# A fused FFT and gated layer on one core: unread products ahead of the tables, another order of the first phase, a padded E row, and joins between VectorE's two products

## The chip, the core and the metric

The kernel runs on one core of a Trainium2 chip. The metric is the device time of one execution in microseconds. The time before is 1947.34 us, the median of 3 runs (1947.0 to 1948.01). Engines are called TensorE (PE in the profile; PEld is its weight load), VectorE (DVE), ScalarE (ACT), GpSimd (POOL) and SyncE (SP, which issues most DMAs here).

## The reference

```python
# x: (8, 3008, 256) float32; weights float64 as numpy makes them: gate, val (256, 1536), out (1536, 256)
X = np.fft.fft(np.fft.fft(x, axis=1), axis=2).real.astype(np.float32)
x = X.reshape(24064, 256)
gate = 1.0 / (1.0 + np.exp(-(x @ w_gate)))
val = x @ w_val
out = (gate * val @ w_out).astype(np.float32)
```

## The kernel before

**What it computes.** The real part of the two-dimensional transform is cos·cos minus sin·sin. The kernel takes the sums over the 3008 rows as products with cosine and sine tables (`stab`), and folds the transform over the 256 columns (`dtab`) into the weights. Rows `k` and `3008 - k` share the same sums, so only 1505 positions are computed, as `pk` (cosine sums of the folded columns), `qk` (sine sums) and one row `E` (cosine sums of the middle column, 128). All matmuls are float32, and each shows as two records in the trace.

**The first phase (L767 to L817, batch 0).** SyncE issues the loads in this order: two weight pieces, the two halves of `x`, the four pieces of the tables (cosine for `q` 0 to 2 and 3 to 5, then the sines), then weight pieces 2, 3, 5, 6, 8, 9, 4 and 7. The weights arrive as 64-bit floats. `weight_parts` (L299, L300 on ScalarE), `weight_join` (L309, L310 and L312 on VectorE, then L314 on GpSimd) turn a piece into float32. `merge` multiplies a piece of `w_gate` or `w_val` with `dtab` on TensorE (tile `ps`), and ScalarE copies the result to `G2` and `G1` (L334, L335). Small DMAs take the first row of `G2` to `ge` (L337). VectorE folds `x` (`fold_ops`, L391 to L404). TensorE then makes the cosine sums in two blocks of positions (tiles `ev` and `od`, blocks 0 and 1), the sums of E (`pe`) and the sine sums. For each block `then` copies `ev` to SBUF on ScalarE (L493), and `places` adds and subtracts on VectorE (L498, L501). For E, L550, L551 and L556 on ScalarE and four instructions on VectorE build `er`, which goes to memory (`ed`, L560).

**The loop (L883 on).** It has 576 tiles: 8 batches, 6 chunks of up to 252 positions, 12 blocks of 128 hidden units. The order of all instructions is written out by hand (a manual schedule). In step `i`:

- `front_a(i)`: TensorE adds `G1`·`pk` for gate and value to a PSUM bank `pf`. For `i` below 5 it also adds E by a product of one row (`G2[0:1]` with `er`, L608); for later tiles ScalarE has written `ge`·E into the bank first (`seed`, L599).
- `gate_a(i-1)`: the first sigmoid (L628) and the values of the mirrored positions, `z` (L629).
- `part(i)`: ScalarE saves twice the bank (L614, tile `ae`).
- `gate_b(i-1)`: VectorE's first product (L641), the second sigmoid (L642) and VectorE's second product (L643), which releases the bank; later GpSimd adds blocks of `h` (L649).
- the lists `pre[i]` (joins of a piece, then `weight_parts` of the next) and `use[i]` (`merge` on TensorE), for `i` up to 12.
- `back`, from `i` = 5 on: TensorE multiplies a finished block with `w_out` (tile `po`).
- `front_b(i)`: TensorE adds `G2`·`qk` to the bank, after L614 has read it.

There are three PSUM banks for `pf`; five others hold `po`, and in the first phase `ev`, `od`, `pe` and most `ps`. The joins of a step stand behind that step's second product; `insert(0, ...)` makes piece 4 precede piece 10 in step 4, and piece 7 precede piece 11 in step 5:

```python
        if i:
            gate_b(i - 1)
        for f in pre.pop(i, []) + use.pop(i, []):
            f()
```

The products of `merge` with piece 10 stand in step 5, between `front_a(5)` and the first `back`. The tile `wqk` (tag "qk") is the second buffer of the tag of `qk`; until batch 1 needs it, it holds weight pieces 3 and 5.

Of the kernel before, what the change touches and what calls it, by code (L numbers as in the profile page):

```python
# [82 lines left out]
def kernel(  # L83
# [10 lines left out]
    nc = tc.nc  # L94
    B, _, _, _, D = xf.shape
    F = moe_w_gate.shape[1]
    P = 128
# [8 lines left out]
    CH = 252  # L106
    NB = 1 + max(b // 3 for b in PLACE)
    WC = 256
# [12 lines left out]
    pqp = ctx.enter_context(tc.tile_pool(name="pqp", bufs=2))  # L121
# [12 lines left out]
    def mm(o, l, r, start, stop):  # L134
        nc.tensor.matmul(o, l, r, start=start, stop=stop, skip_group_check=True)  # L135

    def bank(name, other=None):
        if other is not None:
            return pso.tile([P, 512], F32, name=name, tag=f"po{other}")
        return psx.tile([P, 512], F32, name=name, tag="x")  # L140
# [37 lines left out]
    dt = const.tile([P, 2, D], F32, name="dt")  # L178
# [3 lines left out]
    G2 = const.tile([P, 2, F], F32, name="G2")  # L182
# [59 lines left out]
    shared = {}  # L242
    KEEP = 10

    def weight_load(j):


        w, c = jobs[j]
        src = (moe_w_gate, moe_w_val, moe_w_out)[w]
        src = src[2 * c * P : 2 * (c + 1) * P, :] if w == 2 else src[:, c * WC : (c + 1) * WC]  # L250
        src = src.rearrange("(c p) f -> p c f", p=P)

        def some(n, pool, tag):

            if tag not in shared:
                shared[tag] = pool.tile([P, n * WC], F32, name=f"w{tag}", tag=tag)
            return shared[tag]

        def home(j):

            if j in (0, 1, 2, 3, 5):
                if j > 2:
                    ws = some(4, pqp, "qk")[:, (j // 5) * 2 * WC : (j // 5 + 1) * 2 * WC]
                    return sp.tile([P, 4 * WC], F32, name="raw", tag="sf"), ws
                t = hp.tile([P, 6 * WC], F32, name="raw", tag="h")
                return t[:, 0 : 4 * WC], t[:, 4 * WC :]
            if j in (4, 6, 9):
                t = wf[:, {4: 1, 6: 2, 9: 3}[j]].rearrange("p m n -> p (m n)")
                return t[:, 0 : 4 * WC], t[:, 4 * WC : 6 * WC]
            t = some(10, cp, "c")  # L270
            if j == 7:
                raw = pqp.tile([P, 4 * WC], F32, name="raw", tag="pk")
                return raw, t[:, 6 * WC : 8 * WC]
            return t[:, 0 : 4 * WC], t[:, 4 * WC : 6 * WC]

        if j < KEEP:
            raw, ws = home(j)
        else:
            both = some(24, xp, "x4").rearrange("p (i n) -> p i n", n=2 * WC)
            r, i = (j - KEEP) % 3 * 2, 6 + (j - KEEP) % 6  # L280
            raw, ws = both[:, r : r + 2].rearrange("p a n -> p (a n)"), both[:, i]
            if w == 2:
                i = (0, 0, 8, 0, 2, 4)[c] * WC
                ws = some(10, cp, "c")[:, i : i + 2 * WC]
        raw = raw.bitcast(I32).rearrange("p (c f w) -> p c f w", c=2, w=2)
        ws = ws.rearrange("p (c f) -> p c f", c=2)
        WS[j] = ws
        if src.dtype == F32:
            nc.sync.dma_start(out=ws, in_=src)
        else:  # L290
            RAW[j] = raw
            nc.sync.dma_start(out=raw.rearrange("p c f w -> p c (f w)"), in_=src.bitcast(I32))

    def weight_parts(j):

        if j in RAW:
            raw, ws = RAW[j], WS[j]
            lo, hi = raw[:, :, :, 0], raw[:, :, :, 1]
            nc.scalar.activation(ws, hi.bitcast(F32), AF.Abs)  # L299
            nc.scalar.activation(lo, lo.bitcast(U32), AF.Copy, scale=2.0 ** -29)  # L300

    def weight_join(j):
        if j not in RAW:
            return
        raw, ws = RAW.pop(j), WS[j]
        lo, hi = raw[:, :, :, 0], raw[:, :, :, 1]
        wi = ws.bitcast(I32)
        ts = nc.vector.tensor_scalar
        ts(out=ws, in0=ws, scalar1=2.0 ** -15, scalar2=HUGE, op0=ALU.max, op1=ALU.min)  # L309
        ts(out=wi, in0=wi, scalar1=3, scalar2=0x3FFFFFF8, op0=ALU.logical_shift_left,  # L310
           op1=ALU.bitwise_and)
        nc.vector.scalar_tensor_tensor(out=wi, in0=hi, scalar=-(2 ** 30), in1=wi,  # L312
                                       op0=ALU.bitwise_and, op1=ALU.bitwise_or)
        nc.gpsimd.tensor_tensor(wi, wi, lo, op=ALU.add)  # L314
# [194 lines left out]
    def seq_start(b):  # L509
        PQE[b] = [pqp.tile([P, NK + 1], F32, name=name, tag=name) for name in ("pk", "qk")]  # L510
        for t in PQE[b]:
            nc.vector.memset(t[:, NK:], 0.0)

    def seq_group(b, blk, what, other=None):
        return half(b, lambda q: W[b, blk][what][:, q, :], PQE[b][what], blk, what == 1, other)
# [12 lines left out]
    E0 = []  # L528
# [47 lines left out]
    def cut(i):  # L576
        b, c, _ = groups[i // 3]
        k0, n = chunks[c]
        f = i % NFT
        return PQE[b], slice(k0, k0 + n), n, f, slice(f * P, (f + 1) * P)  # L580
# [8 lines left out]
    PF, AP, Z = {}, {}, {}  # L589
    N1 = 5  # L590

    def seed(i):

        _, _, n, f, _ = cut(i)
        PF[i] = bank("pf").rearrange("p (g n) -> p g n", g=2)[:, :, 0:n]
        for g in range(2 if i >= N1 else 0):
            nc.scalar.activation(PF[i][:, g], EK[i // NFT], AF.Copy, scale=ge[:, g, f : f + 1])  # L599

    def front_a(i):
        (pk, *_), ks, _, _, fs = cut(i)
        if i < N1:
            seed(i)
        for g in range(2):
            mm(PF[i][:, g], G1[:, g, fs], pk[:, ks], i < N1 and g == 0, True)
        for g in range(2 if i < N1 else 0):
            mm(PF[i][:, g], G2[0:1, g, fs], E0[0][:, ks], False, True)  # L608

    def part(i):  # L610

# [19 lines left out]
    def block(p, i):  # L631

        R = 2 * chunks[groups[p][1]][1] // 3
        return H[p][:, i % 3, i // 3 * R : (i // 3 + 1) * R] if i < 9 else SF[p][:, i - 9, 0:R]

    def gate_b(i):

        n = cut(i)[2]
        p, fh = i // 3, i % 3
        z, h, pf = Z.pop(i), H[p], PF.pop(i)  # L640
        nc.vector.tensor_tensor(h[:, fh, 0:n], h[:, fh, 0:n], pf[:, 1], op=ALU.mult)  # L641
        nc.scalar.activation(pf[:, 0], z[:, 0], AF.Sigmoid)  # L642
        nc.vector.tensor_tensor(h[:, fh, n:], pf[:, 0], z[:, 1], op=ALU.mult)  # L643
        if p < NG:
            return
        if fh == 1:
            SF[p] = sp.tile([P, 8, 2 * CH // 3], F32, name="sf", tag="sf")
        for dst, a, b, op in H_SUMS.get(fh, ()):
            nc.gpsimd.tensor_tensor(block(p, dst), block(p, a), block(p, b),  # L649
                                    op=(ALU.subtract, ALU.add)[op])  # L650
# [134 lines left out]
    weight_use(1)  # L785
    seq_start(0)

    qs = tuple(range(NQ // 2)), tuple(range(NQ // 2, NQ))
    cos = [seq_group(0, blk, 0, (2 * blk, 2 * blk + 1)) for blk in range(2)]
    e_, e_even = e_sums(1)  # L790
    for i, (f, q) in enumerate(zip(fold_ops(0, NQ // 2), qs)):
        f()
        if i:
            e_(*q)
        cos[0][0](*q)
        if not i:
            e_(*q)
        cos[1][0](*q)
    cos[0][1]()()
    rest, last_ = e_even()  # L800
    rest()
    last_()
    cos[1][1]()()
    sin = [seq_group(0, blk, 1, (2 * blk, 2 * blk + 1)) for blk in range(2)]
    for q in qs:
        for sums, _, _ in sin:
# [15 lines left out]
    def at(i, *fs):  # L822
        side.setdefault(i, []).extend(fs)


    pre, use = {}, {}
    for j, i in ((5, 0), (6, 1), (8, 2), (9, 3), (10, 4), (4, 4), (11, 5), (7, 5), (12, 6), (13, 7), (14, 8),
                 (15, 9), (16, 10), (17, 11)):
        if i:
            pre.setdefault(i - 1, []).append(lambda j=j: weight_parts(j))  # L830
        pre.setdefault(i, []).insert(0, lambda j=j: weight_join(j))
        if KEEP <= j < len(jobs) - 3:
            at(i, lambda j=j: weight_load(j + 3))
    for j, i in ((2, 0), (3, 1), (5, 1), (6, 2), (8, 3), (9, 4), (4, 5), (10, 5), (11, 6), (7, 6), (12, 7), (13, 8),
# [48 lines left out]
    for i in range(count):  # L883
        front_a(i)
        if i:
            gate_a(i - 1)
        part(i)
        if N1 <= i + 1 < count:
            seed(i + 1)
        if i:  # L890
            gate_b(i - 1)
        for f in pre.pop(i, []) + use.pop(i, []):
            f()
        if i >= 5:
            back((i - 5) // 3, (i - 5) % 3)
        front_b(i)
        n = 3 if i >= count - 8 else 2 + i % 2
        for f in later[0:n]:
            f()
        del later[0:n]  # L900
        for f in side.pop(i, []):
            f()
    gate_a(count - 1)
    gate_b(count - 1)
    for f in later:
        f()
# [51 lines left out]
```

## Time and profile before

| | value |
|---|---|
| median of 3 runs | 1947.34 us |
| the profiled execution: time, span | 1947.65 us, 1945.9 us |
| TensorE busy, share of the span | 1914.6 us, 98% |
| weight load of TensorE | 1775.4 us, 91% |
| VectorE, ScalarE, GpSimd busy | 1438.5, 1340.9, 1558.8 us |
| mean granted clock of TensorE | 0.996 |
| TensorE busy from 0 to 100 us | 81.14 us |
| TensorE busy from 500 to 1000 us | 500.00 us |

The profile is of one execution, from its first instruction to its last; 1.75 us of the execution's time lie outside the span. Busy time of an engine is the time covered by its instructions. A group such as "PE MATMUL ps" is an engine, an operation and the tile it writes. Waits are put down to what ended last before the waiting instruction could start. The chain of waits is followed back from the last instruction. "PEclk" is the share of full clock that TensorE was granted.

### The profile page before, as it was taken

The numbers are of one execution on the slowest core, as the hardware profiler recorded it, in microseconds if no ns is written. First come the engines' busy times: TensorE is split into PE (matmuls) and PEld (weight loads), VectorE is DVE, ScalarE is ACT, GpSimd is POOL, SyncE is SP. The second block draws the span as 40 slices with busy tenths as digits, with TensorE's granted clock in tenths as the row PEclk, the third lists the DMA queues.
The fourth block names the chain that finished last, engine by engine and source line by source line (L and its number), as shares of the span: only waits on it lengthen the run. The fifth ranks groups of instructions, "written<-read, shape, count | busy, mean of one in ns | idle before, by whom it ended". The sixth has DMA issues, their size and how long they took to land.

```text
span 1945.9 us, 34331 instructions
## 1 busy us (share of the span) xinstructions
PE 1914.6 (98%) x11180; PEld 1775.4 (91%) x11180; DVE 1438.5 (74%) x3240; ACT 1340.9 (69%) x3142; POOL 1558.8 (80%) x2795
## 2 busy tenths in 40 slices
PE   7999999999999999999999999999999999999997
PEld 4689889999999999999999999999999999999997
DVE  5576787777776877778777777777777777767776
ACT  3677757776777677776777767777677766777774
POOL 1269989997889788986889879888788886777776
PEclk9999999999999999999999999999999999999999
DMA  8153512212022121212112021111200100011011
GB/s 306 50 149 21 122 48 82 52 22 79 14 52 55 32 62 20 71 30 79 17 38 66 14 82 25 47 46 24 83 14 15 24 17 15 15 23 18 15 19 27
DMA packets 172122, 96.91 MB, mean 50 GB/s; under 512 B 136106, under 2 KB 164012, under 8 KB 169396
## 3 DMA queue, kind: packets, MB, share of 16 engines
q1 hardware_dynamic: 169842, 94.06, 20.1%
q8 instruction: 90, 1.47, 0.3%
q10 hardware_dynamic: 2070, 0.65, 0.2%
q14 instruction: 88, 0.72, 0.1%
q0 software_dynamic: 32, 0.00, 0.0%
HBM read 69.96 MB, written 46.71 MB: 60 GB/s over the span
## 4 chain that ended last, share of the span: by engine, by line
PE 95%; DVE 3%; DMA 1%; ACT 1%; issue 0%; SPq 0%; DVEq 0%; ACTq 0%
PE pf L135 49%; PE po L135 41%; PE ev L135 3%; PE ps L135 1%; DVE c L713 1%; PE od L135 1%; DMA st<-in_stab_dram 1%; DVE z L629 0%; ACT pf L642 0%; PE pe L135 0%; DVE h L643 0%; DVE h L641 0%; DVE os L723 0%; DVE er L501 0%; DVE x L431 0%
## 5 line engine op out<-in xcount | busy, mean ns | idle before, releaser
L649 POOL TENSOR_TENSOR sf<-h 128x168 f32<-128x168 f32 (+1 forms) x940 | 521.1, 573 | 219.2 <-DVE h L643 218.8
L649 POOL TENSOR_TENSOR sf<-h,sf 128x168 f32<-128x168 f32 (+1 forms) x1128 | 628.9, 578 | 59.3 <-DVE h L643 59.0
L135 PE MATMUL pf<-qk,G 128*128 128x252 f32 (+1 forms) x2304 | 582.7, 376 | 1.9 <-ACT ae L614 1.9
L135 PE MATMUL pf<-pk,G 128*128 128x252 f32 (+1 forms) x2304 | 582.8, 376 | 0.0
L643 DVE TENSOR_TENSOR h<-pf,z 128x252 f32<-128x252 f32 (+1 forms) x576 | 241.7, 420 | 430.5 <-ACT pf L642 430.5
L599 ACT ACTIVATE pf<-ek,ge 128x252 f32<-128x252 f32 (+1 forms) x1142 | 538.2, 471 | 19.2 <-DMA ge<-G 0.6
L135 PE MATMUL po<-sf,wf 128*128 128x168 f32 (+1 forms) x3008 | 518.8, 305 | 0.0
L614 ACT ACTIVATE ae<-pf 128x504 f32<-128x504 f32 (+1 forms) x576 | 339.6, 590 | 236.0 <-PE pf L135 234.7
L135 PEld LDWEIGHTS pf<-pk,G 128*128 128x128 f32 x2304 | 436.4, 190 | 52.9 <-issue 1.6
L135 PEld LDWEIGHTS po<-sf,wf 128*128 128x128 f32 x3008 | 462.9, 190 | 8.1
L135 PE MATMUL po<-h,wf 128*128 128x168 f32 (+2 forms) x2640 | 469.3, 306 | 0.0
L713 DVE TENSOR_TENSOR c<-c 128x168 f32<-128x168 f32 (+1 forms) x929 | 439.1, 504 | 5.1
L135 PEld LDWEIGHTS pf<-qk,G 128*128 128x128 f32 x2304 | 410.6, 190 | 34.4 <-ACT ae L614 3.5
L135 PEld LDWEIGHTS po<-h,wf 128*128 128x128 f32 x2640 | 420.3, 190 | 17.3 <-issue 0.9
L629 DVE TENSOR_TENSOR z<-ae,pf 128x504 f32<-128x504 f32 (+1 forms) x576 | 383.4, 666 | 32.5 <-ACT h L628 31.0
L628 ACT ACTIVATE h<-pf 128x252 f32<-128x252 f32 (+1 forms) x576 | 217.9, 378 | 161.2 <-PE pf L135 157.0
L642 ACT ACTIVATE pf<-z 128x252 f32<-128x252 f32 (+1 forms) x576 | 214.3, 372 | 95.8 <-DVE h L641 93.1
L641 DVE TENSOR_TENSOR h<-h,pf 128x252 f32<-128x252 f32 (+1 forms) x576 | 232.6, 404 | 0.0
L649 POOL TENSOR_TENSOR sf<-sf 128x168 f32<-128x168 f32 (+1 forms) x188 | 108.6, 578 | 14.7
L649 POOL TENSOR_TENSOR sf<-sf,h 128x168 f32<-128x168 f32 (+1 forms) x188 | 102.4, 545 | 0.0
L690 ACT COPY c<-po 128x504 f32<-128x504 f32 (+1 forms) x141 | 80.2, 569 | 2.3 <-PE po L135 2.3
L723 DVE STREAM_TRANSPOSE os<-c 128x256 f32<-128x256 f32 x192 | 73.7, 421 | 0.7 <-issue 0.6
(133 smaller groups left out, 865.5 us busy)
## 6 DMA issues: line engine op xcount, KB each, us to landing
x<-xr SPq DMA_DIRECT2D x14, 1536.0 KB
out_dram<-os SPq DMA_DIRECT2D x372, 56.0 KB
xr<-in_xf_dram SPq DMA_DIRECT2D x14, 768.0 KB
xr<-in_xf_dram SPq DMA_DIRECT2D x35, 256.0 KB
ek<-ed SPq DMA_DIRECT2D x39, 126.0 KB
out_dram<-os SPq DMA_DIRECT2D x284, 7.0 KB
st<-in_stab_dram SPq DMA_DIRECT2D x4, 1111.9 KB
x<-in_xf_dram SPq DMA_DIRECT2D x2, 1512.0 KB
```

The lines of the kernel that those rows point to most:

```text
L135: nc.tensor.matmul(o, l, r, start=start, stop=stop, skip_group_check=True)
L599: nc.scalar.activation(PF[i][:, g], EK[i // NFT], AF.Copy, scale=ge[:, g, f : f + 1])
L614: nc.scalar.activation(AP[i], PF[i], AF.Copy, scale=2.0)
L628: nc.scalar.activation(H[p][:, fh, 0:n], PF[i][:, 0], AF.Sigmoid)
L629: nc.vector.tensor_tensor(z[:, :, ::-1], AP.pop(i), PF[i], op=ALU.subtract)
L641: nc.vector.tensor_tensor(h[:, fh, 0:n], h[:, fh, 0:n], pf[:, 1], op=ALU.mult)
L642: nc.scalar.activation(pf[:, 0], z[:, 0], AF.Sigmoid)
L643: nc.vector.tensor_tensor(h[:, fh, n:], pf[:, 0], z[:, 1], op=ALU.mult)
L649: nc.gpsimd.tensor_tensor(block(p, dst), block(p, a), block(p, b), op=(ALU.subtract, ALU.add)[op])
L690: (nc.vector.tensor_copy if t == 1 or t == 3 and not last else nc.scalar.copy)(C[0][:, 3 * t * R : 3 * (t + 1) * R], PO[t][:, 0 : 3 * R])
L713: engine.tensor_tensor(t[:, dst * R : (dst + 1) * R], *v, op=(ALU.subtract, ALU.add)[op])
L723: nc.vector.transpose(os_[0][:, s, 0:nb, h, :], t[:, c0 : c0 + nb * TB])
```

## The change

Six edits, all in the first 100 us of the program:

1. Ten products `dt`·`dt` (128x128 by 128x256) into a bank that nobody reads are put between the merges of pieces 0 and 1 and the first cosine sums.
2. In the second half of the fold, the cosine sums of block 0 come ahead of the sums of E; they did so in the first half already.
3. The copy and placing of block 1's cosine sums (L493, L498, L501) come ahead of the work on E; they stood behind it.
4. E's first 252 positions are copied on ScalarE into row 0 of `e0`, a piece of `wqk` of 128 rows that GpSimd has set to zero. The five first tiles multiply all 128 rows of `G2` with `e0`, in place of one row with `er`.
5. In steps 1 to 11 the joins go between VectorE's first and second product, in the order of the list.
6. Piece 4's join moves from step 4 to step 1, and its `weight_parts` from step 3 to step 0.

```diff
-                    ws = some(4, pqp, "qk")[:, (j // 5) * 2 * WC : (j // 5 + 1) * 2 * WC]
+                    ws = some(5, pqp, "qk")[:, (j // 5) * 2 * WC : (j // 5 + 1) * 2 * WC]
...
-            mm(PF[i][:, g], G2[0:1, g, fs], E0[0][:, ks], False, True)
+            mm(PF[i][:, g], G2[:, g, fs], e0, False, True)
...
-    def gate_b(i):
+    def gate_b(i, *between):
...
         nc.scalar.activation(pf[:, 0], z[:, 0], AF.Sigmoid)
+        for f in between:
+            f()
         nc.vector.tensor_tensor(h[:, fh, n:], pf[:, 0], z[:, 1], op=ALU.mult)
...
+    e0 = shared["qk"][:, 4 * WC : 4 * WC + CH]
+    nc.gpsimd.memset(e0, 0.0)
+    warm = bank("warm", 2)
+    for i in range(10):
+        mm(warm[:, 0:WC], dt[:, 0, 0:P], dt[:, 0], True, True)
...
         f()
-        if i:
-            e_(*q)
         cos[0][0](*q)
-        if not i:
-            e_(*q)
+        e_(*q)
         cos[1][0](*q)
     cos[0][1]()()
+    cos[1][1]()()
     rest, last_ = e_even()
     rest()
     last_()
-    cos[1][1]()()
+    nc.scalar.copy(e0[0:1], E0[0][:, 0:CH])
...
-    pre, use = {}, {}
-    for j, i in ((5, 0), (6, 1), (8, 2), (9, 3), (10, 4), (4, 4), (11, 5), (7, 5), (12, 6), (13, 7), (14, 8),
+    pre, use, join = {}, {}, {}
+    for j, i in ((5, 0), (6, 1), (4, 1), (8, 2), (9, 3), (10, 4), (11, 5), (7, 5), (12, 6), (13, 7), (14, 8),
                  (15, 9), (16, 10), (17, 11)):
...
-        pre.setdefault(i, []).insert(0, lambda j=j: weight_join(j))
+        (join if i else pre).setdefault(i, []).append(lambda j=j: weight_join(j))
...
-            gate_b(i - 1)
+            gate_b(i - 1, *join.pop(i, []))
```

## The prediction

> **What bounds the kernel now.** I read the page first. TensorE is busy for 98% of the span and carries 95% of the chain:
>
> ```profile
> span 1945.9 us, 34331 instructions
> PE 95%; DVE 3%; DMA 1%; ACT 1%; issue 0%; SPq 0%; DVEq 0%; ACTq 0%
> ```
>
> So only time in which TensorE waits, runs slowly or does something dearly can be won. By stage, TensorE is busy for 81.1 of the first 100 us and for all of 500 to 1000; the change touches only the first 100. There I followed the chain of waits (start, length, what), from 0 to 100 us:
>
> ```profile
> 3.04 16.10 DMA st<-in_stab_dram
> 19.28 2.85 PE ev L135 x4
> 27.48 1.36 PE pe L135 x12
> 35.26 0.60 DMA ed<-er
> 36.37 1.53 PE ev L135 x4
> 39.17 1.27 PE od L135 x4
> 46.15 2.74 PE pf L135 x12
> 55.29 1.92 PE ps L135 x8
> 68.76 1.40 DVE wx L310
> 72.35 3.68 PE ps L135 x8
> 77.72 1.70 PE pf L135 x8
> 79.42 1.73 PE ps L135 x8
> ```
>
> It shows three losses. The tables land at 19.14 and the sums start at 19.28. The chain leaves TensorE for E's work (35.26) and comes back at 36.37. It leaves again in step 4 for VectorE's joins, and the products of piece 10 start at 72.35, at 3.68 us where the same eight records take 1.73 at 79.42.
>
> The clock explains the slow rows (columns: stretch, length, busy with records, granted clock, DMA share, GB/s; TensorE alone):
>
> ```profile
> 17.00:18.00 1.00, 0.00 (x0) 0.91 0.88 335
> 18.00:19.00 1.00, 0.00 (x0) 0.50 0.84 307
> 24.00:25.00 1.00, 1.00 (x12) 0.68 1.02 239
> 73.00:74.00 1.00, 1.00 (x4) 0.50 0.76 80
> ```
>
> TensorE ends the first merges at 15.08, idles, and its clock halves near 17.8. It comes back near 24.6, 5.4 us after work resumed. After the idle stretch from 68.24 to 72.35 it halves once more until about 75.8.
>
> **The change, part by part.** The sum is against the profiled execution: 1947.65 us, span 1945.9, 0.31 above the median.
>
> *Ten unread products.* 20 records of 128x256, the shape of `ps`: at 1.73/8 = 0.216 they take 4.3 us from 15.08 and end at 19.4, 0.1 after the sums could start. At half clock they would take 8.6 and end at 23.7. I take the first: the clock had been raised by the merges, since it fell only at 17.8, and now nothing lets it fall. The merges themselves ran slow nearly to their end (16 records in 6.65 us), so an earlier or later rise shifts the end by about 2 us at most. From 19.4 everything runs at full clock: 48 records of sums at 1.27/4 = 0.317 are 15.2 us, 24 of `pe` at 1.36/12 are 2.7, together 18.0. If nothing else waits, the sine sums end at 37.4 instead of 42.33: **5.0 us**.
>
> What could wait? VectorE's folds end at 21.2 (block 1, first half), 24.3 and 26.3 (second halves); TensorE would ask for them at 22.7, 24.6 and 27.8. The later tables are 1.14 MB each, and from 20 to 30 us the DMAs moved 278 GB/s, so they land 4.1 us apart: 23.2, 27.3 and 31.4. Wanted: 24.6, 29.7 and 33.5.
>
> The clock's rule can be set against this. The Trainium skill's page "TensorE: Matmul & The Clock Gate" (What's actually happening) says that the clock rises after one busy window of about 3.4 us, in windows that run free of the kernel. By 3.4 us at half clock the old start would lose only 1.7 us, where the trace shows 5.4 us at half clock, a loss of 2.7, and the sum would be 1.0 smaller. I take the trace's row.
>
> *Order of cosines and E.* Moving block 1's copy (L493) and its two placings ahead of E frees the banks that the sines reuse. TensorE's idle 1.64 us before 36.37 go (they are within the 5.0): block 1's `od` would end at 29.7 and be placed by 30.8, when the sines of block 0 are still running until 31.6. The E chain moves behind it. From its second ScalarE copy to the end of the `ed` issue it took 32.15 to 35.85, 3.7 us; now 30.9 to 34.6. Behind that on ScalarE stand the new copy (about 0.37, as L334), piece 2's parts, both sine copies, and pieces 3 and 5. They begin at 35.0 instead of 36.22: ScalarE gains 1.2 us where TensorE gains 5.0. That cover was 3.9 us and is gone. I get piece 2 joined on GpSimd at 38.7 (wanted 39.1) and `qk` placed at 40.7 (wanted 40.8). I charge 0.3, between 0 and 1. The padded products themselves wait for the new copy, done at 35.0 and wanted at 38.2. `ed`, issued 1.2 us earlier, is read back by ScalarE's own queue after piece 5's parts, at about 39.3; the old row has 5.9 us between the two issues and no wait there, the new one 5.2.
>
> *E row padded.* GpSimd's zeroing lies at 11.4, with GpSimd idle until 39. E's products keep their 252 columns; what goes is the change between 1 and 128 rows, seen as weight loads held back:
>
> ```profile
> 43.11 0.72 PEld L135 LDWEIGHTS pf<-er,G 1*128 1x128 f32 x4 [0.33 <-issue]
> 44.15 1.59 PEld L135 LDWEIGHTS ps<-raw,dt 128*128 128x128 f32 x8 [0.33 <-issue]
> ```
>
> Twelve records with E in them take 2.74, at 1.70/8 they would take 2.55; the merge after E 1.92, at 79.42 1.73. That is 0.38 a tile, for five tiles **1.9 us**; without this effect 0.
>
> *Joins.* In step 4 VectorE now joins piece 10 alone, right after L641, and not piece 4, then 10, after L643:
>
> ```profile
> 64.58 0.41 DVE L641 TENSOR_TENSOR h<-h,pf 128x252 f32<-128x252 f32 x1
> 66.45 0.42 DVE L643 TENSOR_TENSOR h<-pf,z 128x252 f32<-128x252 f32 x1 [1.46 <-ACT pf L642]
> 66.79 0.42 DVE L309 TENSOR_SCALAR wf<-wf 128x512 f32<-128x512 f32 x1
> 68.76 1.39 DVE L310 TENSOR_SCALAR wx<-wx 128x512 int32<-128x512 int32 x1
> ```
>
> A join spans 1.55 us (0.42, 0.43, 0.69 and gaps), GpSimd's add 1.3 more. From 65.0 (L641's end) piece 10 is ready at 67.9, before TensorE's 68.24. Before that, piece 4's parts and join sit three steps earlier: on ScalarE behind piece 6's parts, on VectorE behind its join, on GpSimd between the adds of pieces 6 and 8. SyncE's order is untouched; its loads of pieces 10 to 12, which wait for `x` to be free, go out at 37.4 instead of 42.36, so piece 10 is there long before step 3. So the 4.1 us of idle time go, and with them the half clock on the merge (3.68 - 1.73 = 1.95): **6.0 us**. The bounds are 0, if something else holds the merge as long, and 6.0.
>
> What comes late next? On the new clock, step 0 starts at 37.4. A step takes 3 x 0.85 for `pf` and 1.73 for each merge: 4.3, and 6.0 in step 1, which has two. The merge of piece 10 is then due at 37.4 + 4 x 4.3 + 6.0 + 0.85 = 61.4. Step 0 gets piece 4's two parts on ScalarE. Seven weight pieces after the last table, 0.52 MB each at 352 GB/s, land by 31.4 + 7 x 1.5 = 41.9, and ScalarE asks at 41.3; queued behind are L334, L335 and L628 of tile 0, with 2 us to spare before TensorE needs them. In step 1 piece 4's L310 meets GpSimd's add of piece 6, as at 68.76 (1.39, not 0.43). That holds L643 of tile 0 until 48.8; its bank is wanted at 52. In step 5 the pinch is real. ScalarE needs 4.5 us between L614 of step 4 and the L628 after it (64.66 to 69.17, four parts and two copies in between), so L628 stands at 62.6 on the new clock, then L629, L641, the join of piece 11 and GpSimd's add make 67.0; TensorE asks at 66.5: 0.5. For piece 12 the same count gives 0.4. Piece 13 is in time. The old 0.13 at 84.6 goes.
>
> *Sum.* 5.0 + 1.9 + 6.0 - 0.3 - 0.5 - 0.4 + 0.1 = **11.8 us**. After 100 us TensorE waits for 1.9 us in all, on ScalarE, at places fixed by the loop and not by time, so the gain lasts. 1947.65 - 11.8 - 0.31 = 1935.5 us. A measurement here tells 0.2%, 3.9 us.
>
> **The rivals.**
>
> 1. *The clock falls all the same.* If the merges rise early they end near 13, the products near 17.4, and the 1.9 us until 19.28 fall into a mostly idle window. Then the sums start at half clock: 2.7 us lost, 1938.2. For it: the clock fell in a window that had held 0.7 us of work. Against it: in this trace it rose late.
> 2. *Part of the stall in step 4 stays.* The new cover is 0.3 to 0.5 us. If ScalarE is later by 1 to 2 us than my count (its parts wait for piece 4, say), TensorE waits that long in steps 0, 5 and 6, but not long enough to halve the clock: 1.5 to 4 us, 1937 to 1939.5.
> 3. *The products run at half clock* and end at 23.7: 4.3 us given back, 1939.8. Against it: the fall at 17.8.
> 4. *Slower: joins between the two products choke the banks.* L643 releases the `pf` bank. A join there costs 1.55 us, or 2.5 where L310 meets GpSimd (1.39). It decides once L643 comes after the bank is wanted, two steps on. If all 13 joined pieces held TensorE for 1.2 us each, 15.6 would eat the 12.9 and leave 1950. VectorE's step with a join is 0.67 + 0.41 + 0.42 + 2.5 = 4.0 against TensorE's 4.3 to 5.1, so it would need a second delay.
> 5. *The products are not there.* The changed program's instruction order shows all ten on TensorE, behind the merges; I give this nothing.
>
> **How the numbers follow.** Forecast 0.64 (1934 to 1937), the first rival 0.13, the second 0.14, the third 0.04, the slower one 0.04, and 0.01 for about no change. The range runs from 1933.6 (no new pinch, and 0.7 for the joins' earlier end elsewhere) to 1939.6, over the first two rivals. Faster 0.94, same 0.02, slower 0.04.
>
> **What would show it.** Right: `warm` from about 15 to 19.4, clock at 1.00 from 17 to 76, the last sine sum near 37.4, no held weight loads around E, the merge of piece 10 near 61.4 taking 1.73, and short waits of TensorE for GpSimd before the merges of pieces 11 and 12. Wrong: a clock of 0.50 after 19.4, a wait of over 1 us in steps 0 to 5, or a later stage that grows by what the start gave.

## The result, and the profile after

The changed kernel takes 1935.84 us (median of 4 runs, 1935.56 to 1936.26) against 1947.17 us of the kernel before (4 runs). The ratio is 0.9942, with a 95% interval from 0.9924 to 0.9959: 11.3 us less. The forecast was 1935.5. The profiled execution took 1935.95 us with a span of 1934.2.

By the page of the changed kernel 11.7 us of the span are gone, and TensorE still carries 94% of the chain.

TensorE alone, the first 75 us of the changed kernel (start, length, instructions, idle time before them and what ended it):

```profile
13.93 4.48 PE L135 MATMUL warm<-dt 128*128 128x256 f32 x20
18.56 1.53 PE L135 MATMUL ev<-st,x 126*128 126x377 f32 x4 [0.15 <-DVE x L401]
...
39.51 1.99 PE L135 MATMUL ps<-raw,dt 128*128 128x256 f32 x8 [0.68 <-POOL raw L314]
...
62.14 1.89 PE L135 MATMUL ps<-wx,dt 128*128 128x256 f32 x8
...
67.87 1.99 PE L135 MATMUL ps<-wx,dt 128*128 128x256 f32 x8 [0.45 <-POOL wx L314]
```

The unread products end at 18.4, 0.15 us before the sums start. The merge of piece 10, at 72.35 before, starts at 62.14 behind no wait. The clock rows of TensorE alone confirm it: what was 0.50 at 18 us before is 1.00 now (columns as in the prediction: stretch, length, busy with records, granted clock, DMA share, GB/s).

```profile
18.00:19.00 1.00, 0.85 (x4) 1.00 0.91 353
```

By the starts of the same instructions in the two profiles, the gain grows like this:

| mark on TensorE | before | after | gain so far |
|---|---|---|---|
| first sum | 19.28 | 18.56 | 0.72 |
| first `pf` product (sums done) | 42.17 | 36.97 | 5.20 |
| first product of `front_a(5)` | 67.23 | 61.29 | 5.94 |
| first `po` behind that merge | 75.87 | 63.87 | 12.00 |
| merge of piece 11 | 79.26 | 67.87 | 11.39 |
| merge of piece 12 | 84.68 | 73.20 | 11.48 |
| last `po` products | 1928.32 | 1916.41 | 11.91 |

The 0.72 are no work of the change: the tables landed earlier in this execution. Among the profiles below, the first sum starts between 18.56 and 20.05 where nothing but the tables and the fold holds it. The medians of the kernel before, taken again in each session, lie between 1946.99 and 1947.59, so two kernels whose medians differ by less than about 0.5 us are not told apart here.

The chain of waits of the changed kernel shows one thing that was not in the forecast:

```profile
18.42 16.37 DMA raw<-in_moe_w_gate_dram
...
34.87 0.50 ACTq L560
...
35.71 0.67 ACT raw L299
```

The store of E (L560) sits on ScalarE's queue until piece 2 has landed, at 34.8. E itself was ready at 33.8. The copy to `e0` (at 35.40) and piece 2's own parts stand behind it.

### The profile page after: what moved, and what is told of

It is laid out like the page before. It is cut to its first block, busy times and chain, and to the rows that moved or that the text cites. A ratio compares the mean times of both kernels' runs of the same rounds, so it can differ in the third digit from the quotient of the medians.

```text
span 1934.2 us, 34373 instructions
## 1 busy us (share of the span) xinstructions
PE 1911.6 (99%) x11200; PEld 1777.5 (92%) x11200; DVE 1438.1 (74%) x3240; ACT 1340.2 (69%) x3143; POOL 1558.3 (81%) x2796
## 4 chain that ended last, share of the span: by engine, by line
PE 94%; DVE 3%; DMA 2%; ACT 1%; issue 0%; SPq 0%; ACTq 0%; DVEq 0%
PE pf L135 49%; PE po L135 41%; PE ev L135 2%; DVE c L715 1%; DMA raw<-in_moe_w_gate_dram 1%; DMA st<-in_stab_dram 1%; PE ps L135 1%; PE od L135 1%; DVE z L629 0%; ACT pf L642 0%; DVE h L641 0%; DVE h L645 0%; DVE os L725 0%; PE pe L135 0%; DVE x L431 0%
## 5 line engine op out<-in xcount | busy, mean ns | idle before, releaser
L614 ACT ACTIVATE ae<-pf 128x504 f32<-128x504 f32 (+1 forms) x576 | 339.2, 589 | 234.0 <-PE pf L135 233.0
L629 DVE TENSOR_TENSOR z<-ae,pf 128x504 f32<-128x504 f32 (+1 forms) x576 | 383.5, 666 | 35.3 <-ACT h L628 33.8
```

The lines of the kernel that those rows point to most:

```text
L614: nc.scalar.activation(AP[i], PF[i], AF.Copy, scale=2.0)
L629: nc.vector.tensor_tensor(z[:, :, ::-1], AP.pop(i), PF[i], op=ALU.subtract)
```

## The experiments

Each changes one or two things of one of the two kernels. Edit 2, the place of E's sums in the second half of the fold, was not tried apart. Medians are in us; the ratio is to the kernel before, run on the same chip in the same session.

**Without the unread products.**

```diff
-    for i in range(10):
-        mm(warm[:, 0:WC], dt[:, 0, 0:P], dt[:, 0], True, True)
```

> The changed kernel without the ten unread products. My theory: TensorE idles before the tables, its clock halves, and the sums run at half clock for about 5 us; that costs 2.7 us at the sums, of which 1.0 us comes back in step 0, where TensorE waits for ScalarE anyway: 1937.5 us, and the waits for piece 2 in step 0 gone. Rival A: all of the first phase hangs on piece 2's landing near 34.8, so the products are worth under 0.5 us: 1936.2. Rival B: nothing comes back: 1938.5 or more.

Measured: 1937.29 (5 runs, 1936.62 to 1937.94), ratio 0.9951 [0.9937, 0.9964]. In its trace the first sum starts at 18.89 and the first `pf` product at 40.04: 21.15 us for the sums, against 18.41 with the products. The 2.7 us are there. The merge of piece 2 follows without a wait, so about 1 us comes back. The theory holds, with 1.5 us in the medians against the 1.7 expected.

**The unread products alone, on the kernel before.**

> The kernel before with the ten unread products alone. My theory: 2.7 us less, since the sums run at full clock and everything behind them moves forward with them, the idle stretch in step 4 included: 1944.5 us, sums ending near 39.5. Rival: the stretch in step 4 is tied to when ScalarE and the small DMAs get through, not to TensorE, and takes the gain back: 1946.5 to 1947.2, with a longer wait before piece 10's merge.

Measured: 1949.49 (10 runs, 1948.42 to 1951.39), ratio 1.0013 [1.0004, 1.0022]. That is slower than before, which neither theory had. Its chain of waits and its clock (two views):

```profile
18.81 16.15 DMA raw<-in_moe_w_gate_dram
...
35.03 0.61 DMA ed<-er
35.64 0.46 ACT a L493
...
36.15 2.87 PE ev L135 x4
```

```profile
36.00:37.00 1.00, 0.85 (x2) 0.50 1.04 383
42.00:43.00 1.00, 1.00 (x4) 0.85 0.09 35
```

TensorE reaches the sines of block 1 earlier, but their banks come free no earlier. Block 1's copy (L493) stands behind the store of E, and that behind piece 2's landing, an event of the DMAs. E's last placing in this kernel, a view of VectorE:

```profile
32.21 0.53 DVE L501 TENSOR_TENSOR er<-a 1x376 f32<-1x376 f32 x1
```

In the kernel before it ran later, and its end, not piece 2, let the store go at 35.26 (chain of waits):

```profile
34.69 0.54 DVE er L501
```

TensorE idles for 3.9 us instead of 1.6. The clock that the products had saved falls here instead, for 6.8 us, and the first `pf` product starts at 44.97, 2.8 later than in the kernel before. The profiled execution (1950.36) is one of the longer ones: five of the ten lie from 1948.42 to 1949.03, with a mean granted clock of 0.996 or 0.997 on record, and five from 1949.94 to 1951.39 with 0.995 or 0.996. How long the clock is halved in the quicker five was not seen.

**The changed kernel with E ahead of block 1's copy again.**

```diff
     cos[0][1]()()
-    cos[1][1]()()
     rest, last_ = e_even()
     rest()
     last_()
+    cos[1][1]()()
```

> The changed kernel with block 1's copy and placings behind the work on E again; the unread products, the padded row and the joins stay. My theory, formed on the run with the products alone: the order and the products only work together. The store of E (ed) stands on ScalarE's queue and goes out only when piece 2 has landed, near 34.8; block 1's copy waits behind it, TensorE idles 3.9 us from about 32, its clock halves for 6.8 us, and the sines end 8 us later than in the changed kernel, of which 1 us comes back in step 0: 1942.8 us. Rival: the order is worth the 1.6 us of idle time that the old trace shows, and no more: 1937.5.

Measured: 1942.46 (9 runs, 1940.62 to 1943.43), ratio 0.9973 [0.9963, 0.9983]. The explanation of the last run holds in the other kernel too. TensorE waits 4.67 us for L493, the granted clock is 0.50 from 35.1 to 42.0, and `pf` starts at 45.18. This profile too is of a longer execution (1942.9); three of the nine took 1940.62 to 1940.76.

```profile
19.23 16.45 DMA raw<-in_moe_w_gate_dram
...
36.36 0.47 ACT a L493
...
36.87 2.87 PE ev L135 x4
```

**The products, with the store of E on GpSimd's queue, on the kernel before.**

```diff
-                (nc.sync if m > 1 else nc.scalar).dma_start(out=ed[1:] if m > 1 else ed[0:1], in_=er)
+                (nc.sync if m > 1 else nc.gpsimd).dma_start(out=ed[1:] if m > 1 else ed[0:1], in_=er)
```

> The kernel before with the ten unread products, and with the store of E on GpSimd's DMA queue, so that ScalarE does not wait there for piece 2. My theory: block 1's copy runs near 33.9, TensorE idles 2.3 us and not 3.9, the clock mostly holds, and the products pay: 1945 us, against 1949.5 for the products alone. Rival: the wait for piece 2 isn't the cause, the E chain itself is; then the idle time stays near 3.9 us and the time near 1949.

Measured: 1945.42 (10 runs, 1944.5 to 1946.75), ratio 0.9991 [0.9981, 1.0], 4.1 us less than the products alone. L493 starts at 33.02 and TensorE's wait shrinks to 1.12 us:

```profile
32.37 0.54 DVE er L501
...
33.02 0.48 ACT a L493
...
33.54 1.53 PE ev L135 x4
```

The store itself, in the timeline of this kernel:

```profile
33.21 0.52 POOL L560 DMA_DIRECT2D ed<-er  x1 [21.99 <-DVE er L501]
```

With the store out of ScalarE's way the granted clock stays at 1.00 through the whole first phase (it falls at 68.3, ahead of piece 10's merge, whose join stands here as before). The same products that cost 2.5 us bring 2.0, each against the kernel before of its own session, though the interval of the ratio reaches 1.0. So the wait for piece 2's landing, and not the E chain as such, had turned them into a loss. From GpSimd's queue the store goes out at 33.21, ahead of piece 2, whose parts start at 34.94. So the store doesn't need piece 2 for its data; what ties the two on ScalarE's queue no run shows.

**One row again.** E's product as before, without `e0`, its zeroing and its copy.

> The changed kernel with E's product of one row as before (no zeroed tile, no copy). My theory: 0.38 us more for each of five tiles, of which step 0 hides its own because TensorE waits there, and 0.3 us less on ScalarE ahead of piece 2: 1.2 us slower, 1937.0 us; weight loads held by 0.33 us around the one-row products. Rival: the row count costs nothing and the copy only delays ScalarE: 1935.5, faster than the changed kernel.

Measured: 1936.85 (5 runs, 1936.2 to 1937.79), ratio 0.9949 [0.9937, 0.9962]. The weight loads of this kernel, then of the changed one:

```profile
37.96 0.72 PEld L135 LDWEIGHTS pf<-er,G 1*128 1x128 f32 x4 [0.33 <-issue]
39.00 1.59 PEld L135 LDWEIGHTS ps<-raw,dt 128*128 128x128 f32 x8 [0.33 <-issue]
```

```profile
43.10 0.83 PEld L135 LDWEIGHTS pf<-wqk,G 128*128 128x128 f32 x4
43.95 1.05 PEld L135 LDWEIGHTS ps<-wqk,dt 128*128 128x128 f32 x5
```

The three tiles from `front_a(2)` to `front_a(5)` take 14.00 us with one row (48.08 to 62.08) and 12.83 with 128 (48.46 to 61.29): 0.39 a tile, as forecast. In step 0 TensorE doesn't wait for piece 2 in the one-row kernel. It has no copy on ScalarE, but in its profile the store also goes out 0.6 us earlier (34.26, not 34.87), so the trace doesn't separate the two. Its 1.0 us in the medians fits 1.2, at the edge of what can be told.

**The joins as before.**

```diff
-    for j, i in ((5, 0), (6, 1), (4, 1), (8, 2), (9, 3), (10, 4), (11, 5), (7, 5), ...
+    for j, i in ((5, 0), (6, 1), (8, 2), (9, 3), (10, 4), (4, 4), (11, 5), (7, 5), ...
-        (join if i else pre).setdefault(i, []).append(lambda j=j: weight_join(j))
+        pre.setdefault(i, []).insert(0, lambda j=j: weight_join(j))
```

> The changed kernel with the joins as before: behind the second product, later piece first, piece 4 in step 4. My theory: about 4 us of idle time before the merge of piece 10 are back, the clock halves and that merge takes 3.7 us, less the 0.5 us that the new pinch at piece 11 cost: 5.5 us slower, 1941.3 us. Rival: with the earlier start ScalarE and the small DMAs are further ahead, the idle stretch stays under 3 us and the clock holds: 1938 to 1939.

Measured: 1942.91 (10 runs, 1942.04 to 1944.3), ratio 0.998 [0.9971, 0.9989]. TensorE waits 4.3 us before piece 10's merge, which then takes 3.78:

```profile
66.51 3.78 PE L135 MATMUL ps<-wx,dt 128*128 128x256 f32 x8 [4.30 <-POOL wx L314]
```

An earlier start of the phase does not shorten this wait. The loss is 7.1 us, not the 5.5 expected: the granted clock is 0.50 from 65.1 to 71.9 here, 6.8 us and not the 3.4 of the kernel before, so the first `po` behind the merge is slow too (2.79 us, not 1.85).

**Which of the two join edits?** First the old place with piece 4 still early (only the second line of the diff above), then the new place with piece 4 late (only the first).

> The changed kernel with the joins behind the second product and the later piece first, but piece 4 still in step 1. My theory: without piece 4 in the way the join of piece 10 starts behind L643 near 61.1 and ends on GpSimd near 64; TensorE waits 1.9 us for it, too short for the clock to fall, and 1.5 us more for piece 11, which stands behind piece 7: 1938.5 us. Rival: the place between the products decides, and 4 us of idle time with a half clock come back: 1942.

Measured: 1944.11 (10 runs, 1941.89 to 1946.57), ratio 0.9986 [0.9977, 0.9995]. The expected 1938.5 was wrong. Putting each join at the head of the list also put piece 4 ahead of piece 6 in step 1. TensorE waits three times (1.56 us for piece 10 between the two shown), and the last wait halves the clock (`ps` of piece 11 takes 3.25 us in full):

```profile
52.29 1.99 PE L135 MATMUL ps<-wf,dt 128*128 128x256 f32 x8 [2.03 <-POOL wf L314]
...
74.14 2.40 PE L135 MATMUL ps<-wx,dt 128*128 128x256 f32 x6 [2.32 <-POOL wx L314]
```

> The changed kernel with piece 4's join back in step 4, behind piece 10's, both between the two products. My theory: piece 10 comes first either way, so its merge does not wait; piece 4 lengthens ScalarE's step 3 and VectorE's step 4, which delays the join of piece 11 by 1 to 2 us: 1937 us. Rival: moving piece 4 is what removed the idle time: 1940 or more.

Measured: 1936.33 (4 runs, 1936.13 to 1936.9), ratio 0.9945 [0.993, 0.996], not told apart from the changed kernel. Piece 10's merge waits 0.43 us, the first `po` another 0.44 for piece 4, and piece 11's merge not at all. The delay of piece 11 that was expected did not come. So the place between the products, with the list's own order, brings the gain; moving piece 4 brings none that this shows. Place and order were not tried apart. In the run with the joins behind the second product, piece 10 is the only piece joined in step 4, so the order of the list can't have made its wait of 1.56 us, against none in the changed kernel.

**Five and twenty products.**

> The changed kernel with five unread products in place of ten. They end near 16.2 and leave 2.4 us idle before the tables. My theory: a stretch of 2.4 us is too short to halve the clock in most executions (it fell after 4.1 and 3.9 us so far): 1935.8 us, clock 1.00 from 17 to 25. Rival: any window mostly idle halves it, as in the old trace, where the window had held 0.7 us of work: sums at half clock for up to 5 us, 1937.3 us as without products.

Measured: 1936.95 (5 runs, 1935.72 to 1937.65), ratio 0.9943 [0.9929, 0.9956]. Two runs lie with the changed kernel and three with the kernel without products. In the profiled execution (1937.65) TensorE idled 3.07 us, and the clock fell and was back 3.4 us later:

```profile
20.00:21.00 1.00, 1.00 (x3) 0.50 1.01 370
```

My theory that 2.4 us are too short was too simple: the stretch came out longer here, and the clock does fall in some executions. For the two quicker ones there is only the mean granted clock of the whole execution, 0.998, as in three of the four runs of the changed kernel, against 0.997 in the other three. That fits a clock that held, but does not show where.

> The changed kernel with twenty unread products. They end near 22.7 if the clock is full, 4.1 us after the tables have landed. My theory: TensorE is the bound from there, but step 0 waits 1 us for ScalarE anyway, so about 3 us slower: 1938.9 us. Rival: the first phase hangs on piece 2 and the loads, so most of the 4.1 us are hidden: under 1937.

Measured: 1938.83 (4 runs, 1938.53 to 1939.59), ratio 0.9955 [0.9942, 0.9969]. The first sum starts at 22.81, 4.25 later than with ten, and step 0 gives 1 us back. Of 5, 10 and 20 products, ten are the quickest here.

**Two attempts at a faster version.** Both put the store of E on GpSimd's queue and its read-back behind step 0; the second also moves piece 7 from step 5 to step 3.

```diff
-                (nc.sync if m > 1 else nc.scalar).dma_start(out=ed[1:] if m > 1 else ed[0:1], in_=er)
+                (nc.sync if m > 1 else nc.gpsimd).dma_start(out=ed[1:] if m > 1 else ed[0:1], in_=er)
...
-    e_rows(0)
+    at(0, lambda: e_rows(0))      # behind the definition of at
```

> The changed kernel with the store of E on GpSimd's DMA queue (GpSimd is idle there) and its read-back behind step 0. My theory: ScalarE no longer stands 1 us before the store until piece 2 has landed; the copy to e0 and piece 2's parts come 0.9 us earlier and TensorE's wait in step 0 (0.7 us, and 0.3 before the qk products) goes: 1934.9 us. Rival: piece 2's landing bounds its own parts as well, so step 0 waits as before: 1935.8.

Measured: 1936.33 (5 runs, 1935.79 to 1937.31), ratio 0.9942 [0.993, 0.9955]: no gain. ScalarE in the first step of this kernel:

```profile
33.79 0.40 ACT L808 COPY wqk<-er 1x252 f32<-1x252 f32 x1 [0.66 <-DVE er L498]
34.93 0.68 ACT L299 ACTIVATE raw<-raw 128x512 f32<-128x512 f32 x1 [0.74 <-DMA raw<-in_moe_w_gate_dram]
...
43.01 0.68 ACT L299 ACTIVATE wf<-wf 128x512 f32<-128x512 f32 x1 [2.06 <-DMA wf<-in_moe_w_out_dram]
```

The copy and piece 2's parts do come earlier (34.93, not 35.71) and TensorE's wait in step 0 is gone. But ScalarE then stands 2.06 us, not 0.99, before piece 4, whose landing did not move, and with it the copies to `G1` behind it. From the first `pf` product to piece 10's merge TensorE needs 24.99 us instead of 25.17.

> As the run with E's store on GpSimd's queue, and piece 7's join moved from step 5 to step 3 (its parts to step 2), out of ScalarE's full step 4. My theory: L628 of step 4 comes 1.2 us earlier and with it piece 11's join, so TensorE's 0.5 to 0.6 us before that merge go: 1934.4 us. Rival: the same work now delays step 3 (two joins there, piece 9's merge or piece 10's join late by over 0.5 us): no gain, 1935 or more.

Measured: 1937.69 (5 runs, 1937.46 to 1938.13), ratio 0.9949 [0.9937, 0.9962]. The rival holds. VectorE in step 3 of this kernel:

```profile
57.86 1.40 DVE L310 TENSOR_SCALAR wc<-wc 128x512 int32<-128x512 int32 x1
```

Piece 7's L310 meets GpSimd's add of piece 9 and takes 1.40 us. That delays the next step's join, and piece 10's merge waits 1.73 us. Neither version beats the changed kernel.

## Why the prediction was right, point by point

- **The sum.** 11.8 us were forecast, 11.7 measured between the profiled executions, and 0.7 of these are tables that landed earlier. The rest, 11.0, is what is to be compared. That the sum came within 0.1 us is partly luck: the sums brought 0.5 less and step 0 cost 0.9 more than forecast, and the earlier tables and a loss of 0.4 at piece 12 that did not come made up for it. In the table of the time before, TensorE's busy time from 0 to 100 us should read 81.35 us, not 81.14; no term uses it.
- **Full clock in the sums, and their order: 5.0 forecast, 4.5 measured** (5.20 less the 0.72). The products ran at full clock (4.48 us for all). The attribution was wrong, though: the prediction booked the whole 5.0 under the products and only 1.6 of it under the order. The products alone cost 2.5 us, and taking the order back costs 6.6. What failed here is the reading of the old 1.64 us of idle time as the price of the order, whatever the products do. In the old trace that time ended with E itself (placed at 35.23, stored at 35.26). In the run with the products alone E is placed at 32.74, and the store still waits for piece 2 until 35.03. So once E is ready before piece 2 has landed, whatever brings TensorE there sooner lengthens its wait, until the clock falls.
- **Step 0: 0.3 forecast, 1.2 measured** (piece 2's merge starts 0.8 late, the `qk` products and those behind them 0.4 more). The term was mis-sized because the prediction had ScalarE free at 34.6, from the old length of the chain around the store. In the new place that store waits for piece 2, and piece 2, which the count of bytes put at 31.4 + 1.5 = 32.9, lands at 34.8.
- **Padded row: 1.9 forecast.** From the first `pf` product to `front_a(5)` 0.74 us are gained, which is 1.9 less the 1.2 lost in step 0; per tile 0.39 against 0.38.
- **Joins: 6.0 forecast, 6.1 measured** (5.94 to 12.00). The new pinch was named in the right place: 0.5 forecast at piece 11, 0.6 measured. The 0.4 at piece 12 did not come: its merge starts as close behind GpSimd as before. Piece 4's move was listed with this gain, and the run with piece 4 late shows no share of it.
- **Lasting gain.** After 100 us TensorE waits for 1.9 us on L614 in both profiles, and the last products stand 11.9 us earlier. Of the 0.4 us won behind the merge of piece 12, 0.3 come at one place: the `po` products that started 0.3 us late at 95.32 before start without a gap at 83.54 now. No term of the sum had this.
- **Rivals.** The first, the clock falling all the same, is what five products do in some executions; with ten no profile shows it ahead of the sums. Of the second, the wait in step 0 came (1.2 us), but not the stall in step 4. The third is ruled out by the products' 4.48 us. The slower case did not come from the joins; the combination that is slower than before is one that the prediction did not list, products without the new order.

## What to carry to other kernels

Filling an idle stretch pays only as far as the next event that TensorE does not set: find out whether the next wait ends with a transfer before counting what is gained ahead of it. A DMA issue in a compute engine's queue holds up what stands behind it: here ScalarE stood from 33.8, when E was ready, to 34.8. Parts of a change are best tried one at a time and also left out one at a time: here leaving four of them out (the products, the order, the padded row, the joins) costs 1.5, 6.6, 1.0 and 7.1 us in the medians, together more than the 11.3 that all bring.

## What the runs showed of the hardware

The clock's changes keep to a grid. Between recorded changes lie 3.4, 6.8, 34.1 and 47.8 us in the traces, all multiples of 3.41, and the grid lies differently in each execution. The first rise is not on record: the granted clock reads 1.00 from the start, while the first merges run slow. By the length of their 16 records, 5.11 to 6.65 us where 16 x 0.216 would be 3.5, the clock rose about 3 to 6 us after they began; this is an estimate, since each us at half clock lengthens them by half a us. The clock fell after idle stretches of 4.2, 3.9, 3.07 (five products) and even 2.32 us (piece 11 in the run with the joins behind the second product), but not after one of 2.03 us. The Trainium skill's page "TensorE: Matmul & The Clock Gate" (What's actually happening) says that the clock falls after at least one idle window of about 3.4 us. The stretches of 3.07 and 2.32 us are shorter than one step of the grid. By the times of their falls, 19.66 and 74.72, the last 3.41 us before them held about 0.3 and 1.1 us of work, so a window that is only mostly idle was enough here. The same section has the clock rise after one busy window of that length; the half-clock stretches of these traces were one window (3.4 us) or two (6.8 us).

VectorE's L310 takes 0.43 us alone and 1.39 to 1.40 while GpSimd adds the piece before: in the kernel before (68.76), in the changed one (47.75 and 66.71), and in the run with piece 7 in step 3 (57.86).
